# The q projection of two chunks as one Strassen pair, laid around an output projection

## The chip, the cores and the metric

The kernel runs on one core of a Trainium2 chip. A core has a matrix engine (TensorE, PE in the profile; PEld is its weight load), a vector engine (VectorE, DVE), a scalar engine (ScalarE, ACT), a general engine (GpSimd, POOL) and a sync engine (SyncE, SP) that issues most transfers. [...] The metric is the device time of one execution in microseconds, the median of three; lower is better.

## The reference

One transformer layer over 2,048 rows of 1,024 values: attention over a sliding, dilated window of 8 positions, then a gated feed-forward block. Both add to their input.

```python
def _A_ref(x, wqkv, wo):                      # S = 2048, D = 1024, 32 heads of 32
    qkv = (x @ wqkv) -> q, k, v per head
    idx = pos[:, None] - 2 * arange(8)        # the row itself and 7 earlier ones, two apart
    logits = einsum("bhsd,bhswd->bhsw", q, k[idx]) * 32 ** -0.5     # masked before row 0
    o = einsum("bhsw,bhswd->bhsd", softmax(logits), v[idx])
    return o @ wo

def _B_ref(x, w_gate, w_up, w_down):          # F = 3584
    return ((x @ w_gate) * (x @ w_up)) @ w_down

h  = x + _A_ref(layernorm(x), wqkv, wo)
h2 = h + _B_ref(layernorm(h), w_gate, w_up, w_down)
```

Inputs and output are bf16. What the change touches is the q third of `x @ wqkv`, for rows 1024 to 2047.

## The kernel before

The rows are cut into four chunks of 512 (`TC`). For each chunk the normalized rows lie transposed in `lnTs[c]` (128 x 8 x 512); wqkv is in six blocks of 512 columns: blocks 0 and 1 are q, 2 and 3 are k, 4 and 5 are v. One group is eight matmuls of 128x512, and each result is copied out by ScalarE and stored to memory, from where attention gathers it back with heads and positions over the partitions (qD, kD, vD).

```python
    def mm_group(ps, wt, j, rhs):
        for ko in range(KO):                                   # KO = 8
            nc.tensor.matmul(ps[:], lhsT=wt[:, ko, bass.ts(j, 128)], rhs=rhs[:, ko, :],
                             start=(ko == 0), stop=(ko == KO - 1))

    def qkv(c, blocks, last=False):
        for b in blocks:
            for j in range(4):
                ps = psum.tile([128, TC], F32, tag="mm", name=f"ps{c}_{b}_{j}")
                mm_group(ps, wts["qkv", b], j, lnTs[c])
                evac_qkv(c, b * 4 + j, ps)                     # ScalarE copy, store
                bg.step(GROUP_US)
            if last:
                retire()                                       # frees the weight buffer: the next weights load
```

The attention itself runs on VectorE, as a generator. A small planner, `bg`, puts pieces of it between the matmul groups while the program is written: each `yield` says what the piece is thought to cost, and `bg.step` hands out as much as a group of matmuls takes (`GROUP_US` is 1.73). So the order of the instructions on VectorE is fixed in the program; when they run depends on the chip.

```python
    def attention(c):
        while c and c - 1 not in over:
            yield "later", 1.0
        qD, kD = qkv_in["q", c], qkv_in["k", c]
        lg = att.tile([128, W, SUB], F32, tag="lg", name=f"lg{c}")
        for wp in range(W // 2):
            prod = att.tile([128, 2, DH, SUB], BF, tag="prod", name=f"prod{c}_{wp}")
            for j in range(2):
                o = HB - DIL * (2 * wp + j)
                nc.vector.tensor_tensor(prod[:, j], qD[:], kD[:, :, o:o + SUB], ALU.mult)
                yield 2.3
            # ... five folds of prod into the logits lg
        # ... softmax over lg; products with vD, summed into oD
        nc.gpsimd.dma_start(od[c].rearrange("c g d s -> (c g) d s"), oD[:])
        oT = att.tile([128, KO, 4, SUB], BF, tag="oT", name=f"oT{c}")
        for cp in range(4):
            nc.gpsimd.dma_start(oT[:, :, cp, :], od[c][cp].rearrange("(hg hl) d s -> (hl d) hg s", hl=4))
        oTs[c] = oT
        over.add(c)
        # ... loads for the next chunk
```

The output projection of chunk 0 multiplies oT by wo, adds the input rows and takes the second norm, on VectorE; chunk 1 does the same through `wo_norm`, which has the norm on ScalarE.

```python
    def wo_ln2(c, at={}):
        # ... norm(t): normalize(hs[t]) on VectorE, then a transposing DMA into lnT
        for t in range(4):
            for hf in range(2):
                ps = psum.tile([128, 512], F32, tag="mm", name=f"wo{c}_{hf}_{t}")
                # ... eight matmuls: oT by wo
                nc.vector.tensor_tensor(hs[t][:, bass.ts(hf, 512)], ps[:], hs[t][:, bass.ts(hf, 512)], ALU.add)
                if hf == 1:
                    stats(hs[t], mv4, t)                       # two bn_stats, one bn_aggr
                    rstd_of(mv4, rs4, t, t + 1)
                    bg.spend(1.5)
                elif t > 0:
                    norm(t - 1)
        # ...
```

The main line of this part, in order:

```python
    qkv(0, range(1, 4))                     # block 0 of chunk 0 was done at the start
    load_qk(0)
    bg.finish(rows2)
    for t in range(4):
        norm1[2].transpose(t)
    xtiles[3] = load_x(3, "x", nc.sync)
    pump(6)
    # ...
    start_attention(0)
    # ...
    qkv(1, range(4))
    qkv(0, range(4, 6))
    load_v(0)
    # ...
    qkv(1, range(4, 6))
    start_attention(1)
    pump(pair_at)
    qkv(2, range(6))
    start_attention(2)
    hss[0] = load_x(0, "h", nc.sync)
    qkv(3, range(4), last=True)
    bg.finish(atts[0])
    # ...
    nxt = wo_ln2(0)
    qkv(3, range(4, 6), last=True)
    start_attention(3)
    # ...
    hT0 = ffn1_first(nxt[0], {(4, 2): wo_1})                   # gate and up products; output projection 1 inside
```

The feed-forward part of chunks 2 and 3 already uses this scheme of seven products (`pair_block`), and so do the down products; they are not changed.

Of the kernel before, what the change touches and what calls it, by code (L numbers as in the profile page):

```python
# [18 lines left out]
D = 1024  # L19
# [59 lines left out]
def kernel(  # L79
# [46 lines left out]


# [72 lines left out]
    def load_x(c, what, eng):  # L200
        tiles = []
        for t in range(4):
            xt = hp.tile([128, D], BF, tag="h", name=f"{what}{c}_{t}")
            eng.dma_start(xt[:], x[bass.ds(c * TC + t * 128, 128), :])
            tiles.append(xt)
        return tiles
# [52 lines left out]
    class NormOnScalar(Norm1):  # L259
# [16 lines left out]
        def devs(self):  # L276
            nc.scalar.activation(self.nm, self.s, ACTF.Copy, scale=-1.0 / D)
            for t in range(4):
                nc.scalar.activation(self.junk[:], self.xs[t][:], ACTF.Square, bias=self.nm[:, t:t + 1],
                                     accum_out=self.ss[:, t:t + 1])  # L280
                yield "later", self.pace
            nc.scalar.activation(self.rs4[:], self.ss, ACTF.Ln, bias=eps[:], scale=1.0 / D)
# [17 lines left out]
        def rows(self):  # L300
            for t in range(4):
                self.row(t)
                self.transpose(t)
                yield "later", self.pace

# [33 lines left out]

    qkv_in = {}  # L340

    def evac_qkv(c, m, ps):
        sg = t1k.tile([128, HB + TC], BF, tag="t1k", name=f"sg{c}_{m}")
        nc.scalar.copy(sg[:, HB:HB + TC], ps[:])  # L344
# [5 lines left out]
        if m < 8:  # L350
            nc.sync.dma_start(qd[c][:, 4 * hg:4 * hg + 4, :, :].rearrange("c g d s -> (g d) c s"),
                              sg[:, HB:HB + TC].rearrange("p (c s) -> p c s", c=4))
# [81 lines left out]
    def qkv(c, blocks, last=False):  # L434
        for b in blocks:
            for j in range(4):
                ps = psum.tile([128, TC], F32, tag="mm", name=f"ps{c}_{b}_{j}")
                mm_group(ps, wts["qkv", b], j, lnTs[c])
# [9 lines left out]
    def load_qk(c):  # L448
        qD = att.tile([128, DH, SUB], BF, tag="qD", name=f"qD{c}")
        kD = att.tile([128, DH, SUB + HB], BF, tag="kD", name=f"kD{c}")  # L450
        nc.gpsimd.dma_start(qD[:], qd[c].rearrange("c g d s -> (c g) d s"))
# [98 lines left out]
    class Norm2(NormOnScalar):  # L550
# [11 lines left out]
        def finish(self):  # L562
            yield from self.devs()
# [5 lines left out]
    def wo_norm(c):  # L569
# [4 lines left out]
        for t in range(4):  # L574
            for hf in range(2):
# [6 lines left out]
                if hf == 0 and t > 0:  # L582
                    n.sum(t - 1)
                bg.step(GROUP_US)
        n.sum(3)
        retire(2)
        return n

    def wo_ln2(c, at={}):
        lnT = lnTp.tile([128, KO, TC], BF, tag="lnT", name=f"lnT2_{c}")  # L590
        hs = hss[c]
        mv4, rs4 = ln_tiles(f"2_{c}")

        def norm(t):
            ln = normalize(hs[t], mv4, rs4, t)
            nc.sync.dma_start_transpose(lnT[:, :, bass.ts(t, 128)], ln[:])

        for t in range(4):
            for hf in range(2):
                ps = psum.tile([128, 512], F32, tag="mm", name=f"wo{c}_{hf}_{t}")  # L600
                for kk in range(KO):
                    nc.tensor.matmul(ps[:], lhsT=oTs[c][:, kk, t, :], rhs=wts["wo", c, hf][:, kk, :],
                                     start=(kk == 0), stop=(kk == KO - 1))
                nc.vector.tensor_tensor(hs[t][:, bass.ts(hf, 512)], ps[:], hs[t][:, bass.ts(hf, 512)], ALU.add)
                if hf == 1:
                    stats(hs[t], mv4, t)
                    rstd_of(mv4, rs4, t, t + 1)
                    bg.spend(1.5)
                elif t > 0:
                    norm(t - 1)  # L610
                    bg.spend(0.55)
                bg.spend(0.7)
                if 2 * t + hf in at:
                    at[2 * t + hf]()
                bg.step(GROUP_US)
        norm(3)
        retire(2)
        for t in range(4):
            rows = hsd[c][:, t, :]
            nc.sync.dma_start(rows, hs[t][:, D - rows.shape[-1]:D])  # L620
        return lnT, hs

    ones = const.tile([128, 128], BF)
    nc.vector.memset(ones[:], 1.0)

    class Scale:
        def __init__(self, name, n):
            self.name, self.n = name, n  # L630
            self.l1 = const.tile([128, n], F32, name="l1" + name)
            self.rowb = const.tile([128, 1], BF, name="rowb" + name)

        def add(self, k, src, junk):
            nc.scalar.activation(junk, src, ACTF.Abs, accum_out=self.l1[:, k:k + 1])

        def rows(self):
            row = small.tile([128, 1], F32, tag="l1row", name="row" + self.name)
            nc.vector.tensor_reduce(row[:], self.l1[:], mybir.AxisListType.X, ALU.add)
            nc.vector.tensor_copy(self.rowb[:], row[:])  # L640

        def total(self, ps=None):
            n = TC if ps else 64
            ps = ps or psum.tile([128, TC], F32, tag="mm", name="l1ps" + self.name)
            nc.tensor.matmul(ps[:, 0:n], lhsT=ones[:], rhs=self.rowb[:].to_broadcast((128, n)), start=True, stop=True)
            tot = const.tile([128, 1], F32, name="tot" + self.name)
            nc.vector.tensor_copy(tot[:], ps[:, 0:1])
            eb = const.tile([128, 1], I32, name="eb" + self.name)
# [705 lines left out]
```

## Time and profile before

| | |
|---|---|
| time, median of 3 runs | 770.61 us (770.46 to 770.74) |
| span of the profiled execution | 768.7 us, 10,302 instructions |
| TensorE clock granted | 1.000 |
| TensorE busy | 762.8 us, 3,663 matmuls |
| VectorE busy | 606.0 us |
| ScalarE busy | 513.1 us |
| transfers | 144.85 MB, mean 188 GB/s |

The page of a profile lists the busy time of each engine, the chain of work that ended last (followed back from the last instruction, at each step to what released it), and groups of like instructions. In a group's line stand the source line, the engine, the operation, what is written and read, shapes and count, then busy time and mean duration of one, then the idle time before them and who ended it. A timeline row has the start, the duration, the engine and line, the operation, and in square brackets the idle time before it with what ended that. In the chain, pieces have a start, a length, an engine and a tile. In a list of waits, each line says who waited for whom: total, times, longest. A matmul's row shows 0.38 us because matmuls overlap; the distance between two of them is what counts.

### The profile page before, as it was taken

The numbers are of one execution on the slowest core, as the hardware profiler recorded it, in microseconds if no ns is written. First come the engines' busy times: TensorE is split into PE (matmuls) and PEld (weight loads), VectorE is DVE, ScalarE is ACT, GpSimd is POOL, SyncE is SP. The second block draws the span as 40 slices with busy tenths as digits, with TensorE's granted clock in tenths as the row PEclk, the third lists the DMA queues.
The fourth block names the chain that finished last, engine by engine and source line by source line (L and its number), as shares of the span: only waits on it lengthen the run. The fifth ranks groups of instructions, "written<-read, shape, count | busy, mean of one in ns | idle before, by whom it ended". The sixth has DMA issues, their size and how long they took to land.

```text
span 768.7 us, 10302 instructions
## 1 busy us (share of the span) xinstructions
PE 762.8 (99%) x3663; PEld 350.7 (46%) x3663; DVE 606.0 (79%) x718; ACT 513.1 (67%) x979; POOL 142.5 (19%) x152
## 2 busy tenths in 40 slices
PE   8999999999999999999999999999999999999998
PEld 5444444444444444444444444444444444444444
DVE  5639999999999999999998997975454444568863
ACT  4648966423687398778899986736777677788240
POOL 0000000200002000020000001018778677600000
PEclk9999999999999999999999999999999999999999
DMA  8999796999966699579559448674342423730001
GB/s 268 272 257 260 207 269 153 279 305 283 301 219 216 210 299 294 172 246 326 194 186 300 139 155 279 126 198 107 80 110 55 110 74 91 257 126 29 0 29 55
DMA packets 190915, 144.85 MB, mean 188 GB/s; under 512 B 81808, under 2 KB 181136, under 8 KB 188688
## 3 DMA queue, kind: packets, MB, share of 16 engines
q1 hardware_dynamic: 180416, 116.94, 54.2%
q0 software_dynamic: 3584, 22.02, 8.4%
q10 hardware_dynamic: 6864, 5.24, 2.5%
q8 instruction: 28, 0.46, 0.2%
q14 instruction: 23, 0.19, 0.1%
HBM read 110.10 MB, written 27.26 MB: 179 GB/s over the span
## 4 chain that ended last, share of the span: by engine, by line
PE 97%; DVE 2%; DMA 1%; issue 0%; ACTq 0%; DVEq 0%
PE ps L431 21%; PE dx L944 6%; PE pz L826 6%; PE pwu L431 6%; PE pu L431 6%; PE py L826 6%; PE pwg L431 6%; PE pg L431 6%; PE px L826 6%; PE wo L998 4%; PE pv L826 3%; PE ez L944 3%; PE ey L944 3%; PE ex L944 3%; PE dy L944 3%; PE wo L578 2%
## 5 line engine op out<-in xcount | busy, mean ns | idle before, releaser
L431 PE MATMUL ps<-lnT,w_qkv 128*128 128x512 bf16 x736 | 159.5, 379 | 0.0
L431 PEld LDWEIGHTS <-w_qkv 128*128 128x128 bf16 x736 | 71.9, 98 | 86.1 <-issue 0.2
L344 ACT CAST sg<-ps 128x512 bf16<-128x512 f32 x96 | 55.2, 586 | 46.9 <-PE ps L431 41.6
L477 DVE TENSOR_TENSOR prod<-qD,kD 128x4096 bf16<-128x4096 bf16 x32 | 72.2, 2284 | 12.8 <-DMA kD<-kd 12.8
L523 DVE TENSOR_TENSOR pv<-vD,at 128x4096 bf16<-128x4096 bf16 x32 | 72.4, 2285 | 0.2
L826 PEld LDWEIGHTS <-sw 128*128 128x128 f16 x448 | 43.8, 98 | 52.9 <-issue 0.2
L431 PEld LDWEIGHTS <-w_wu 128*128 128x128 bf16 x448 | 43.8, 98 | 52.9
L431 PEld LDWEIGHTS <-w_wg 128*128 128x128 bf16 x448 | 43.8, 98 | 52.9
L826 PE MATMUL px<-lnT,ws 128*128 128x512 bf16 x224 | 55.2, 379 | 0.0
L536 POOL DMA_DIRECT2D od<-oD x4 | 2.2, 544 | 275.6 <-DVE oD L534 275.6
L431 PE MATMUL pg<-lnT,w_wg 128*128 128x512 bf16 x224 | 52.9, 379 | 0.0
L431 PE MATMUL pu<-lnT,w_wu 128*128 128x512 bf16 x224 | 52.9, 379 | 0.0
L431 PE MATMUL pwu<-lnT,w_wu 128*128 128x512 bf16 x224 | 52.9, 379 | 0.0
L431 PE MATMUL pwg<-lnT,w_wg 128*128 128x512 bf16 x224 | 52.9, 379 | 0.0
L826 PEld LDWEIGHTS <-ws 128*128 128x128 f16 x336 | 32.9, 98 | 39.6
L807 POOL TENSOR_TENSOR sw<-ws 128x512 f16<-128x512 f16 x26 | 30.0, 1155 | 82.4 <-PE pv L826 49.1
L944 PEld LDWEIGHTS <-gs 128*128 128x128 f16 (+1 forms) x280 | 27.4, 98 | 33.0
L479 DVE TENSOR_TENSOR prod<-prod 128x4096 bf16<-128x4096 bf16 x16 | 36.6, 2288 | 0.4
L843 ACT COPY py<-px 128x512 f32<-128x512 f32 x28 | 16.0, 570 | 27.7 <-PE px L826 27.7
L808 POOL TENSOR_TENSOR sw<-sw,ws 128x512 f16<-128x512 f16 x26 | 30.0, 1154 | 2.0
L810 POOL TENSOR_TENSOR sw<-ws,sw 128x512 f16<-128x512 f16 x26 | 30.3, 1167 | 0.0
L809 POOL TENSOR_TENSOR sw<-ws 128x512 f16<-128x512 f16 x26 | 30.1, 1156 | 0.0
(334 smaller groups left out, 1472.9 us busy)
## 6 DMA issues: line engine op xcount, KB each, us to landing
w_wg<-in_B_w_gate_dram SPq DMA_DIRECT2D x14, 1024.0 KB, 6.9
w_wu<-in_B_w_up_dram SPq DMA_DIRECT2D x14, 1024.0 KB, 6.3
w_pair<-in_B_w_gate_dram SPq DMA_DIRECT2D x14, 512.0 KB, 4.0
w_pair<-in_B_w_up_dram SPq DMA_DIRECT2D x14, 512.0 KB, 5.3
w_wo<-in_A_wo_dram SPq DMA_DIRECT2D x6, 1024.0 KB, 7.6
w_qkv<-in_A_wqkv_dram SPq DMA_DIRECT2D x5, 1024.0 KB, 11.5
kd<-sg SPq DMA_DIRECT2D x32, 144.0 KB, 4.4
kD<-kd POOLq DMA_DIRECT2D x4, 1152.0 KB, 8.6
```

What stands on the lines that cost most here:

```text
L344: nc.scalar.copy(sg[:, HB:HB + TC], ps[:])
L431: nc.tensor.matmul(ps[:], lhsT=wt[:, ko, bass.ts(j, 128)], rhs=rhs[:, ko, :], start=(ko == 0), stop=(ko == KO - 1))
L477: nc.vector.tensor_tensor(prod[:, j], qD[:], kD[:, :, o:o + SUB], ALU.mult)
L479: nc.vector.tensor_tensor(prod[:, :, 0:16], prod[:, :, 0:16], prod[:, :, 16:32], ALU.add)
L523: nc.vector.tensor_tensor(pv[:, j], vD[:, :, o:o + SUB], at[:, w, None, :].to_broadcast((128, DH, SUB)), ALU.mult)
L807: eng.tensor_tensor(sw[:, i, 0], a21, a22, ALU.add)
L808: eng.tensor_tensor(sw[:, i, 1], sw[:, i, 0], a11, ALU.subtract)
L809: eng.tensor_tensor(sw[:, i, 2], a11, a21, ALU.subtract)
L810: eng.tensor_tensor(sw[:, i, 3], a12, sw[:, i, 1], ALU.subtract)
L826: nc.tensor.matmul(ps[:], lhsT=lhs[:, ko, :], rhs=rhs[:, ko, :], start=(fresh and ko == 0), stop=(ko == 3), skip_group_check=not fresh)
L944: nc.tensor.matmul(ps[:, bass.ds(lo, n)], lhsT=lhs[k][:, bass.ts(q, 128)], rhs=rhs[k][:, bass.ds(lo, n)], start=(fresh and k == 0), stop=( ...
L998: nc.tensor.matmul(ps[:], lhsT=oTs[c][:, kk, t, :], rhs=wts["wo", 2, hf][:, kk, :], start=(kk == 0), stop=(kk == KO - 1))
```

## The change

A product of two matrices, each cut into 2 x 2 blocks, needs eight block products; Strassen's scheme (here in Winograd's form) needs seven and some sums. The change computes the q projection of chunks 2 and 3 together in that way: the blocks of the weights are q columns m and 4 + m (blocks 0 and 1 of wqkv, `r`) by halves of the contraction (`kh`), and the blocks of the rows are chunks 2 and 3 by the same halves. Its aim is to save TensorE one eighth of these matmuls.

- The q weights are brought into f16 with a power-of-two scale (`Scale`, from a sum of absolute values over the weights), and sums of their blocks are made (`q_weight_sums`), all while chunk 0 and chunk 1 are projected. Chunk 1's q uses the scaled weights as well, so the order of chunk 1 becomes k, then q.
- Loads that stood beside the gather of attention 0's keys (transposes of chunk 2, rows of chunk 3, the v weights) are moved behind it: a tiny GpSimd copy makes the x load wait for kD, and qD waits for the transposes of chunk 1.
- Sums of the rows of chunks 2 and 3 (`q_row_sums`) are made on VectorE right behind attention 0; the last of them, T3, inside the pair, in a weight buffer (`room_q`).
- Half of the pair (m 0 and 1) is put in front of output projection 0, the other half behind it, with pieces of the last value block between its products.
- The norm after output projection 0 goes from VectorE to ScalarE (`wo_norm(0, devs=False)`; `wo_ln2` is removed).
- The total for another scale (`total_h1`) is taken two steps later in output projection 2.

```diff
+    def q_convert():
+        for r in range(2):
+            wt = wts["qkv", r]
+            nc.vector.tensor_scalar(f16(wt[:]), wt[:], scale_q.s, None, ALU.mult)
+        bg.spend(2.6)
+        bg.add(q_weight_sums(), bg.now)
+    def q_weight_sums():
+        for m in range(4):
 ... (a11, a12, a21, a22: the four f16 blocks of m; s1 to s4: rooms of 128x512)
+            nc.vector.tensor_tensor(s1, a21, a22, ALU.add)
+            nc.vector.tensor_tensor(s2, s1, a11, ALU.subtract)
+            nc.vector.tensor_tensor(s3, a11, a21, ALU.subtract)
+            nc.vector.tensor_tensor(s4, a12, s2, ALU.subtract)
+            yield 1.7
+    def q_row_sums():
+        while 0 not in over:
+            yield "later", 0.5
 ...
+        for k in range(4):
+            nc.vector.tensor_tensor(t1[k], b12[:, k, :], b11[:, k, :], ALU.subtract)
+            nc.vector.tensor_tensor(t2[k], b22[:, k, :], t1[k], ALU.subtract)
+            if k % 2:
+                yield 1.7
+        for k in range(4):
+            nc.vector.tensor_tensor(t4[k], b21[:, k, :], t2[k], ALU.subtract)
+        yield 1.7
+        def last_sum(room):
 ... (t3: a view of half of room)
+            nc.vector.tensor_tensor(t3, b22, b12, ALU.subtract)
+            bg.spend(1.3)
+    def q_product(ps, lhs, rhs, fresh):
+        for ko in range(4):
+            nc.tensor.matmul(ps[:], lhsT=lhs[:, ko, :], rhs=rhs[ko], start=(fresh and ko == 0), stop=(ko == 3),
+                             skip_group_check=not fresh)
+        bg.step(GROUP_US / 2)
+    def q_pair(m0, room, between=()):
 ... (out_scalar: ScalarE, scaled, and store; out_vector: VectorE, scaled plus p5, and store)
+        for i in two:
+            xb[i] = bank("x", i)
+            q_product(xb[i], a11[i], b11, True)
+            yb[i] = bank("y", i)
+            nc.scalar.copy(yb[i][:], xb[i][:])
+        for i in two:
+            v = bank("v", i)
+            q_product(v, sw[i][0], t1, True)
+            p5[i] = room[:, i, :]
+            nc.scalar.activation(p5[i], v[:], ACTF.Copy, scale=inv)
+        if m0 == 0:
+            qsum["t3"] = qsum["t3"](room)
+        t3 = qsum["t3"]
+        for i in two:
+            q_product(yb[i], sw[i][1], t2, False)
+            zb[i] = bank("z", i)
+            nc.scalar.copy(zb[i][:], yb[i][:])
+        for f in between[0:1]:
+            f()
+        for i in two:
+            q_product(xb[i], a12[i], b21, False)
+            out_scalar(2, m0 + i, xb[i])
+            q_product(zb[i], sw[i][2], t3, False)
+            ub[i] = bank("u", i)
+            nc.scalar.copy(ub[i][:], zb[i][:])
+            out_vector(3, 4 + m0 + i, zb[i], p5[i])
+        for f in between[1:2]:
+            f()
+        for i in two:
+            q_product(yb[i], sw[i][3], b22, False)
+            out_vector(3, m0 + i, yb[i], p5[i])
+            q_product(ub[i], a22[i], t4, False)
+            out_scalar(2, 4 + m0 + i, ub[i])
-    qkv(0, range(1, 4))
-    load_qk(0)
+    qkv(0, [1, 2], at={(1, 1): lambda: q_abs(0), (1, 2): lambda: q_abs(2), (1, 3): lambda: q_abs(1),
+                       (2, 0): lambda: q_abs(3), (2, 2): scale_q.rows})
+    qkv(0, [3], at={(3, 2): scale_q.total, (3, 3): q_convert})
+    load_qk(0, after=lnTs[1][:, 0, TC - 1:TC])
+    start_attention(0)
+    qkv(1, [2])
     bg.finish(rows2)
+    xtiles[3] = load_x(3, "x", nc.sync, after=qkv_in["k", 0][:, 0, 0:1])
+    pump(6)
+    state["live"] += 1
     for t in range(4):
         norm1[2].transpose(t)
 ...
-    qkv(1, range(4))
+    qkv(1, [3, 0, 1])
 ...
-    qkv(2, range(6))
+    qkv(2, range(2, 6))
+    rows_q = q_row_sums()
+    bg.add(rows_q, bg.now, first=True)
+    qkv(3, [2, 3], last=True)
+    hss[0] = load_x(0, "h", nc.sync)
+    state["live"] += 1
+    qkv(3, [4], last=True)
+    bg.finish(atts[0])
+    bg.finish(rows_q)
+    room_q = wpool.tile([128, 4, TC], F32, tag="w", name="room_q")
+    q_pair(0, room_q)
 ...
+    norm2 = [wo_norm(0, devs=False)]
+    norm2.append(norm2[0].finish(devs=False))
+    bg.add(norm2[1], bg.now, first=True)
+    qkv(3, [5], js=(0, 1))
+    q_pair(2, room_q, between=(lambda: qkv(3, [5], js=(2,)), lambda: qkv(3, [5], last=True, js=(3,))))
+    bg.finish(norm2[1])
```

`q_abs` sums absolute values of half a q block: halves 0 and 1 by a VectorE reduce (128x2048 to 128x1), 2 and 3 on ScalarE. Not shown: the bodies of `Scale` (moved, not changed), the loop parameters `at` and `js` of `qkv`, and the pace of `abs_down`, which goes from 4.9 to 3.9 groups.

## The prediction

> **What bounds the kernel now.** I read the page's share table first, then the chain of work that ended last, then that chain between 20 and 200 us, and last VectorE's timeline and waits around the first attention.
>
> ```profile
> PE 762.8 (99%) x3663; PEld 350.7 (46%) x3663; DVE 606.0 (79%) x718; ACT 513.1 (67%) x979; POOL 142.5 (19%) x152
> ...
> PE 97%; DVE 2%; DMA 1%; issue 0%; ACTq 0%; DVEq 0%
> ```
>
> ```profile
> 27.20 136.41 PE ps L431 x632
> 163.61 13.81 PE wo L602 x64
> 177.42 13.81 PE ps L431 x64
> 191.24 1.73 PE pg L431 x8
> ```
>
> TensorE holds 97% of the chain, and from 27.2 to 191.2 us (the stretch that the change rewrites) it never waits: 632 matmuls in 136.41 us are 0.2158 us each, and each 64 after them take 13.81 us, the same rate. So every matmul removed here is worth 0.2158 us, and every wait put in here costs its full length.
>
> VectorE is the second engine to watch, because attention lives on it:
>
> ```profile
> 39.02 0.55 DVE L192 TENSOR_SCALAR ln<-x,mv,rs 128x1024 bf16<-128x1024 bf16 x1 [1.64 <-ACT sg L347]
> 52.34 2.29 DVE L477 TENSOR_TENSOR prod<-qD,kD 128x4096 bf16<-128x4096 bf16 x1 [12.77 <-DMA kD<-kd]
> ```
>
> ```profile
> 134.26 2.29 DVE L534 TENSOR_TENSOR oD<-oD,pv 128x4096 bf16<-128x4096 bf16 x1
> 136.59 2.29 DVE L477 TENSOR_TENSOR prod<-qD,kD 128x4096 bf16<-128x4096 bf16 x1
> ```
>
> The reader is to see two things. VectorE is idle for 12.77 us before attention 0, until the gathered keys (kD) land. From 52.34 us on it runs attention 0 without a pause worth naming and ends it at 136.6: 84.25 us. Nothing on TensorE sets that end; the landing of kD does.
>
> ```profile
> 44.12 0.54 POOL L452 DMA_DIRECT2D kD<-kd  x1 [12.56 <-DMA kd<-sg]
> ```
>
> That load is issued at 44.12 us, when the last key block has been stored, and lands 8.2 us later.
>
> [...]
>
> **The change part by part.**
>
> Matmuls. The plain q projection of chunks 2 and 3 is 2 chunks x 8 blocks x 8 matmuls = 128. The pair computes four m, each in 7 products of 4 matmuls = 112. That is 16 fewer, 16 x 0.2158 = 3.45 us. The scale adds one 64-column matmul; a 128-column one takes 1.50 / 24 = 0.06 us in the chain. Net -3.39 us. All else on TensorE is the same work in another order, so without a new wait the answer would be 770.61 - 3.39 = 767.2.
>
> Preparation on VectorE, put into the idle stretch. [...] Behind the last norm come five tiny operations (about 0.8 us), two conversions of 128x4096 (1.28 us each by the row of the later gate/up conversion, 2.5 together) and 16 sums of 128x512. Independent ones follow each other at 4.78 / 14 = 0.34 us (row of 14 f16 sums at 441.58), one that reads the result just before it at about 0.45; four groups make 5.9. That is 9.2 us into a hole of 12.8. But the two ScalarE sums (1.9 us each by the row of the same operation on w_ring) push ScalarE's evacuations and norm factors about 2 us late, so the last norm ends at 40.0 rather than 39.5, and the weight sums at about 49.2.
>
> Start of attention 0. The last key block is stored about 1.7 us later than before, for the same ScalarE reason; its landing and kD's are quicker, because transposes, x and weight loads are now held behind kD. I take 1.2 us off the landing of that store and 2.2 off kD's 8.2, both guesses: 44.1 + 1.7 - 1.2 = 44.6 for the issue, and 6 us more, 50.6. So attention 0 starts at max(49.2, 50.6), say 50.3, some 2 us earlier than before, and ends at 50.3 + 84.25 = 134.5.
>
> The row sums. In the order of the built program VectorE does, behind attention 0: one product of attention 1 (2.24), the twelve 128x512 row sums of T1, T2, T4 (4.55), then a product (2.3), a fold (2.32), four smaller folds (1.26, 1.26, 0.72, 0.35), another product (2.24), and only then T3 (128x2048, 1.25). T1, T2 and T4 are there at 134.5 + 6.8 = 141.3. T3 is there 18.5 us behind attention 0, at 153.0.
>
> When TensorE wants them. Counting the matmuls in the new order from the same start, the first product of the pair begins at 143.0, the one with T1 at 144.7, the one with T2 at 146.4 and the one with T3 (the z product) at 149.0. T1, T2 and T4 are in time by 3 us. T3 is not: 153.0 - 149.0 = 4.0 us of wait. I lower it to 3.5, as VectorE's start could be up to a microsecond earlier.
>
> Output projection 0 comes at 155.2 instead of 163.6. Its oT follows the end of attention 0 by some 15 us (store 4.2, four gathers issued over 3.55, up to 7.5 to land), so 149.5: in time. Its own weights are loaded earlier too.
>
> Norm 2 of chunk 0 moves from VectorE (8 bn_stats at 0.65 and 4 norms at 0.5, about 7 us) to ScalarE. There, between 173 and 189 us, ScalarE has two sums over the last rows (2.6), four rows of 1.24 us, and the pair's copies and outputs of about 0.57 to 0.69 each. I follow them in order to a last row at about 188.5 and its transpose landed near 192; the gate products want it at 187.9 plus the 3.5 of above, 191.4. Expected loss 0.4 us, from nothing to 1.5.
>
> Attention 1 ends about 2 us later than before (row sums, T3 and the pair's outputs on VectorE, 4.6 + 1.3 + 8 x 0.70, less the 7 us that left, less the earlier start), near 239. Before, it ended at 237.4 and the first gather landed well before 253.4; now the first is due by about 251 and wanted at 250.0 + 3.5. Just in time.
>
> Sum: -3.39 + 3.5 + 0.4 = +0.5, or 771.1. I round to 771.0.
>
> **The rivals.** (1) No new wait: T3 comes in time, 767.2. For it: the order of the change is plainly laid out to keep kD's way free, and ScalarE's and VectorE's new work fits into measured holes. Against it: attention 0 would have to start at 46 us, while the weight sums alone keep VectorE until 49. (2) The wait is longer, or a second one joins it: kD lands no earlier than before (52.3), which makes the wait for T3 6 us, or the norm rows on ScalarE make the first gate product wait 1.5 to 2 us more. Then 772 to 774. For it: ScalarE is the only engine that gets both the norm and the pair's copies. Against it: a long wait for T3 gives slack to everything behind it. (3) The fifth weight block, now loaded behind kD, comes late for its matmuls at 67 us (issue near 54, 12.5 us to land as before). That would not add up: TensorE would only wait there instead of for T3, as VectorE goes on meanwhile.
>
> **Range and chances.** The end is set by T3, which is set by attention 0's start: 49.0 to 52.3 makes the wait 2.6 to 6 us, the time 769.8 to 773.2, and the norm rows add up to 1.5. I give rival 1 about 15%, and a wait of under 2 us another 15%. Predicted 771.0, 768.0 to 773.5. Two per cent are 15.4 us, more than four times what is removed, and no wait I see is near that: 0.98 within 2%.
>
> **What would show it.** The page should have 15 fewer matmuls (3,648). VectorE's timeline should show weight sums up to about 49, the first attention product at 50, its end near 134.5 and the 128x2048 subtraction ending near 153. TensorE's timeline should show one gap of 2 to 5 us ahead of a z product at 149, released by VectorE, and perhaps a small one at the first gate product, released by the transposing DMA. I am wrong if TensorE runs through 149 without a gap, if the first gap comes at the first gate product or at output projection 1, or if attention 0 starts before 48 or after 52.

## The result, and the profile after

| | before | after |
|---|---|---|
| time, median (four runs each) | 770.56 us (770.46 to 770.74) | 777.69 us (776.51 to 779.00) |
| ratio of the times | | 1.0093, 95% interval 1.0075 to 1.0110 |
| span of the profiled execution | 768.7 us | 775.9 us |
| first gate product starts | 191.07 us | 198.29 us |
| from there to the end | 577.6 us | 577.6 us |
| attention 1's output sent (od) | 237.41 us | 246.03 us |

The change saves its 16 matmuls and costs 7.1 us all the same, against the 0.5 us that the prediction added up. The last row but one places it: behind the first gate product the two executions are equally long, so everything happens before 198 us. The later total of the other scale, which the change also moves, therefore costs or brings nothing that can be seen.

The page of the changed kernel, busy time and the chain of work that ended last:

```profile
PE 759.5 (98%) x3592; PEld 349.8 (45%) x3648; DVE 622.1 (80%) x750; ACT 535.6 (69%) x1013; POOL 144.3 (19%) x154
...
PE 76%; DVE 3%; ACT 1%; issue 1%; DVEq 0%
```

The weight loads (PEld) count 3,648, the predicted number of matmuls (some matmul records are missing from this trace). VectorE has 16 us more to do than before, ScalarE 22 us. In the kernel before TensorE had 97% of the chain; now the chain passes through VectorE and ScalarE too. (The second line adds up to 81%, so part of the chain is not named there, and its 76 can't be set against the 97.) TensorE's list of waits says where (who waited for whom; total, times, longest, in us):

```profile
PE qz L945 <- DVE room_q L932: 6.9, 1, 6.9
...
PE ps L482 <- ACT halo L401: 0.8, 1, 0.8
PE qy L945 <- ACT qy L977: 0.5, 1, 0.5
...
PE ps L482 <- ACT room_q L982: 0.3, 1, 0.3
```

The first is the wait for T3 that the prediction had, at twice its size. VectorE's timeline of the changed kernel, the end of the weight sums, the start of attention 0, its last addition, and T3, followed by the row of GpSimd that asks for kD:

```profile
48.40 0.42 DVE L911 TENSOR_TENSOR qs<-w_qkv,qs 128x512 f16<-128x512 f16 x1
53.94 4.49 DVE L533 TENSOR_TENSOR prod<-qD,kD 128x4096 bf16<-128x4096 bf16 x2 [5.11 <-DMA kD<-kd]
...
135.80 2.29 DVE L590 TENSOR_TENSOR oD<-oD,pv 128x4096 bf16<-128x4096 bf16 x1
...
155.51 1.22 DVE L932 TENSOR_TENSOR room_q<-lnT 128x2048 f16<-128x2048 bf16 x1
```

```profile
46.77 0.54 POOL L508 DMA_DIRECT2D kD<-kd  x1 [9.13 <-DMA kd<-sg]
```

The weight sums end at 48.8 as predicted, and then VectorE stands idle for 5.1 us: kD is asked for at 46.8 and lands at 53.9. Attention 0 takes 84.2 us from there, and T3 ends 18.6 us behind it, both as predicted, so T3 is out at 156.7 and not at 153.0. The chain between T3 and the gate product (start, length, who, how many):

```profile
155.60 1.14 DVE room_q L932
156.79 1.89 PE qz L945 x4
158.68 1.47 PE qx L945 x4
160.15 0.86 PE qz L945 x4
...
198.46 1.73 PE pg L482 x8
```

Four matmuls take 0.86 us; the first four behind the wait take 1.89, the next four 1.47. That is 1.6 us more, and the table of stretches of the same kernel shows why (stretch, its length, TensorE's busy time and matmuls, granted clock, share of the DMA engines, GB/s):

```profile
150.00:152.00 2.00, 0.00 (x0) 1.00 1.20 330
152.00:154.00 2.00, 0.00 (x0) 0.74 1.08 241
154.00:156.00 2.00, 0.00 (x0) 0.50 1.13 272
156.00:158.00 2.00, 1.21 (x3) 0.50 1.04 348
158.00:160.00 2.00, 2.00 (x7) 0.55 0.99 357
160.00:162.00 2.00, 2.00 (x11) 1.00 1.13 346
```

TensorE goes idle at 149.9, its granted clock falls from 1.00 to 0.50 at about 153, and it comes back some 3 us after work has started again: 3.1 us from the start of the wait to the half clock, and 3.0 us back.

The account of the span then reads: 3.4 us saved; 6.9 for T3; 1.6 for the clock; 0.8 at 111 us, where TensorE waits for ScalarE to copy a result out of one of the kernel's eight accumulator tiles (`psum`), as ScalarE stood still for 6.55 us up to 110; 1.2 between 178 and 190, where ScalarE is behind. That is +7.1, and the spans differ by 7.2.

### The profile page after: what moved, and what is told of

It is laid out like the page before. It is cut to its first block, busy times and chain, and to the rows that moved or that the text cites. A ratio compares the mean times of both kernels' runs of the same rounds, so it can differ in the third digit from the quotient of the medians.

```text
span 775.9 us, 10279 instructions
## 1 busy us (share of the span) xinstructions
PE 759.5 (98%) x3592; PEld 349.8 (45%) x3648; DVE 622.1 (80%) x750; ACT 535.6 (69%) x1013; POOL 144.3 (19%) x154
## 4 chain that ended last, share of the span: by engine, by line
PE 76%; DVE 3%; ACT 1%; issue 1%; DVEq 0%
PE dx L1088 6%; PE pz L830 6%; PE pwu L482 6%; PE pu L482 6%; PE py L830 6%; PE pg L482 6%; PE pwg L482 6%; PE px L830 6%; PE wo L647 4%; PE wo L1142 4%; PE pv L830 3%; PE ez L1088 3%; PE ey L1088 3%; PE ex L1088 3%; PE dy L1088 3%; PE ev L1088 2%
## 5 line engine op out<-in xcount | busy, mean ns | idle before, releaser
L482 PE MATMUL ps<-lnT,w_qkv 128*128 128x512 bf16 x595 | 131.7, 379 | 1.8 <-ACT halo L401 0.8
L482 PEld LDWEIGHTS <-w_qkv 128*128 128x128 bf16 (+1 forms) x608 | 59.3, 98 | 72.4 <-issue 1.7
L396 ACT CAST sg<-ps 128x512 bf16<-128x512 f32 x72 | 41.7, 587 | 19.0 <-PE ps L482 9.3
L830 PE MATMUL px<-lnT,ws 128*128 128x512 bf16 x212 | 53.1, 379 | 0.6
L482 PE MATMUL pwg<-lnT,w_wg 128*128 128x512 bf16 x219 | 52.3, 379 | 0.2
L811 POOL TENSOR_TENSOR sw<-ws 128x512 f16<-128x512 f16 x26 | 29.9, 1152 | 86.3 <-PE pv L830 52.7
```

The source lines that it names most:

```text
L830: nc.tensor.matmul(ps[:], lhsT=lhs[:, ko, :], rhs=rhs[:, ko, :], start=(fresh and ko == 0), stop=(ko == 3), skip_group_check=not fresh)
```

## The experiments

Each is the changed kernel with one edit, timed beside the kernel before. This table has what the discussion below rests on: the four TensorE waits (at the z product, which is for T3 except for the 0.3 us of e14 to e17; at the qy product of the second half, for ScalarE; at the first gate product, for a transposed row; at output projection 1, for attention 1's output), and when attention 0 starts, the first gate product starts and attention 1's output is sent. Times are medians, the rest is from the profiled executions.

| run | time (us) | ratio to before, 95% | z | qy | gate | proj. 1 | att. 0 | gate at | output 1 |
|---|---|---|---|---|---|---|---|---|---|
| before | 770.56 | | | | | | 52.3 | 191.1 | 237.4 |
| after | 777.69 | 1.0075 to 1.0110 | 6.9 | 0.5 | 0 | 0 | 53.9 | 198.3 | 246.0 |
| e1 | 775.93 | 1.0050 to 1.0102 | 0 | 2.3 | 4.5 | 0 | 54.1 | 198.1 | 247.3 |
| e2 | 775.70 | 1.0046 to 1.0079 | 0.5 | 0.5 | 0 | 0 | 54.0 | 196.9 | 244.7 |
| e3 | 779.88 | 1.0102 to 1.0132 | 6.4 | 0.5 | 0 | 0 | 56.0 | 201.2 | 249.0 |
| e4 | 775.06 | 1.0042 to 1.0075 | 4.9 | 0.5 | 0 | 0 | 51.0 | 195.4 | 243.1 |
| e5 | 774.48 | 1.0030 to 1.0060 | 0 | 1.9 | 3.6 | 0 | 51.9 | 193.2 | 241.1 |
| e6 | 792.98 | 1.0272 to 1.0308 | 6.5 | 0 | 0 | 6.1 | 52.0 | 196.3 | 253.0 |
| e7 | 790.09 | 1.0231 to 1.0262 | 0 | 1.1 | 0 | 8.7 | 52.7 | 189.1 | 248.1 |
| e8 | 773.89 | 1.0026 to 1.0055 | 0 | 0.8 | 3.6 | 0 | 51.7 | 193.0 | 241.1 |
| e9 | 774.18 | 1.0037 to 1.0062 | 0 | 2.1 | 3.6 | 0 | 53.5 | 194.9 | 243.0 |
| e10 | 776.89 | 1.0071 to 1.0102 | 6.9 | 0.5 | 0 | 0 | 52.1 | 198.0 | 245.7 |
| e11 | 774.58 | 1.0039 to 1.0064 | 0 | 0.7 | 3.6 | 0 | 51.6 | 192.8 | 242.0 |
| e12 | 782.14 | 1.0131 to 1.0177 | 0 | 2.1 | 0 | 4.4 | 52.3 | 191.4 | 245.4 |
| e13 | 777.27 | 1.0065 to 1.0099 | 0 | 1.7 | 2.3 | 3.3 | 53.7 | 193.6 | 247.5 |
| e14 | 781.83 | 1.0125 to 1.0176 | 0.3 | 2.5 | 0 | 5.6 | 51.7 | 192.5 | 247.0 |
| e15 | 781.06 | 1.0124 to 1.0154 | 0.3 | 0.5 | 0 | 5.5 | 51.6 | 189.7 | 244.9 |
| e16 | 781.43 | 1.0113 to 1.0149 | 0.3 | 0.5 | 0 | 5.5 | 54.8 | 190.9 | 246.0 |
| e17 | 781.09 | 1.0120 to 1.0152 | 0.3 | 0.5 | 0 | 5.5 | 51.4 | 189.8 | 244.9 |
| e18 | 772.27 | 1.0013 to 1.0026 | 0 | 2.7 | 0 | 0 | 52.1 | 192.3 | 232.6 |

### Is it T3, the clock, or kD? (e1 to e4)

e1 moves T3 to its place right behind T1 and T2, in other memory:

```diff
+        t3at = f16(att.tile([128, W, SUB], BF, tag="at", name="t3at")[:].rearrange("p w s -> p (w s)"))
+        t3 = [t3at[:, bass.ts(k, TC)] for k in range(2)]
+        t3 += [t1k.tile([128, TC], F16, tag="t1k", name=f"qt3_{k}")[:] for k in range(2)]
+        for k in range(4):
+            nc.vector.tensor_tensor(t3[k], b22[:, k, :], b12[:, k, :], ALU.subtract)
 ... (last_sum and its call inside the pair are taken out)
```

> T3 (b22 - b12, the operand of the z product) is computed right behind T1 and T2 in other memory, ahead of attention 1's pieces on VectorE, nothing left out. Theory (the z product waits for T3, and the clock drops because of that wait): T3 is out near 145.5, well before TensorE wants it at 149.9; the wait of 6.9 us and the slow qz and qx products (1.6 us) both go, 769.2 us (768.2 to 770.5). Rival A (most of the loss lies elsewhere, in ScalarE's norm and the loads, and the wait only moves to a later product): 773 to 777 us, with a new TensorE wait of some us after 150. Rival B (the wait goes, the slow clock stays): 770.8 us.

775.93 us: the wait for T3 is gone and almost nothing is won. Rival A held: 2.3 us now stand at the qy product, 4.5 at the first gate product, and that product starts at 198.1 as in the changed kernel. Part of it is my edit: ScalarE sat idle 8.8 us until 163 for a staging tile (a `t1k` buffer), and e1 uses two of these for T3. e5 mends that.

e2 puts 30 matmuls that nobody reads into the wait:

```diff
+            if m0 == 0 and i == 0:
+                fill = bank("f", 0)
+                for _ in range(30):
+                    nc.tensor.matmul(fill[:], lhsT=a11[0][:, 0, :], rhs=b11[0], start=True, stop=True)
             q_product(zb[i], sw[i][2], t3, False)
```

> The changed kernel with 30 matmuls of 128x512 (0.2158 us each, 6.5 us) whose product nobody reads, put just ahead of the z product, where TensorE otherwise stands idle for 6.9 us. Theory (the qz and qx products behind the wait are slow because an idle TensorE is granted a lower clock): those groups come back to 0.86 us, 776.1 us (775.5 to 776.8) though 30 matmuls more are computed. Rival (they are slow because of what they read, or because of the instruction queue): 777.7 us or more, groups still 1.5 to 1.9 us.

775.70 us, and the two stretches that stood at half clock, from the same table for e2:

```profile
156.00:158.00 2.00, 1.45 (x8) 1.00 1.02 358
158.00:160.00 2.00, 2.00 (x11) 1.00 1.00 343
```

30 matmuls more make the kernel 2.0 us faster by the medians (the ranges of the two overlap by 0.6 us), and the granted clock is 1.00 where it was 0.50 and 0.55: the slow products were the clock, and the clock was the wait. The gate product starts 1.35 us earlier than in the changed kernel.

e3 takes away what holds q's load back, `load_qk(0)` in place of `load_qk(0, after=...)`; this was my explanation of kD's late landing.

> The changed kernel with the load of q of chunk 0 not held back until chunk 1's transposes are in; all else equal. Theory (kD lands at 53.9 instead of 50.6 because the 1 MB of q moves at the same time as the stores of k): q moves near 31 to 37, kD lands at 50.5 to 51.5, attention 0 and T3 are 2.5 to 3.4 us earlier, the wait at 149.9 shrinks to 3.5 to 4.4 us, 774.5 us (773.8 to 775.3). Rival (kD is late because ScalarE evicts k late): kD lands after 53, 777 to 778 us.

779.88 us: the theory fell, and in the other direction. Attention 0 starts at 56.0, later than in any other run. TensorE's list of waits for e3:

```profile
PE qz L945 <- DVE room_q L932: 6.4, 1, 6.4
PE ps L482 <- ACT halo L401: 1.9, 1, 1.9
PE ps L482 <- DMA lnT<-ln: 1.3, 1, 1.3
```

The third line is new. With q's load let loose, chunk 1's transposes come late, TensorE waits for them, and the stores of k follow TensorE. The gate protects kD's way; it doesn't block it.

e4 leaves two of the four sums of absolute values out of the scale, those on ScalarE:

```diff
-    scale_q = Scale("q", 4)
+    scale_q = Scale("q", 2)
-    qkv(0, [1, 2], at={(1, 1): lambda: q_abs(0), (1, 2): lambda: q_abs(2), (1, 3): lambda: q_abs(1),
-                       (2, 0): lambda: q_abs(3), (2, 2): scale_q.rows})
+    qkv(0, [1, 2], at={(1, 1): lambda: q_abs(0), (1, 3): lambda: q_abs(1),
+                       (2, 2): scale_q.rows})
```

> The changed kernel with the scale taken from two half blocks alone: ScalarE's two sums of absolute values (2.1 us each) are left out of the computation. Theory (these sums push ScalarE's evictions of k, and so the stores and kD, by about 2 us): kD lands at 51.5 to 52.3, 775.7 us (775.0 to 776.5). Rival (kD is set by the q load[...]): kD within 0.5 us of 53.9, 777.2 to 778 us.

775.06 us. GpSimd's row for e4:

```profile
44.46 0.54 POOL L508 DMA_DIRECT2D kD<-kd  x1 [8.64 <-DMA kd<-sg]
```

kD is asked for at 44.5 in place of 46.8, and attention 0 starts at 51.0: here kD comes nearly as the prediction wanted it. So ScalarE's two sums make kD late, as e4's theory had it. By how much, one trace can't tell. Thirteen profiled executions (after and twelve of the runs) have the same instructions up to here, and attention 0 starts anywhere from 51.7 to 54.8 in them; in the four whose four sums are all on VectorE (e8, e11, e15, e17) it starts at 51.4 to 51.7. So the sums cost kD anything from next to nothing to some 3 us; why equal programs differ by that much is not shown. And where it starts at 53.5 or later, the wait at 111 us is 0.65 to 2.1 us; where it starts before 52.7, it is 0.4 or nothing. The change makes the x load wait for kD, so the transposes of chunk 3 do, and ScalarE, which has a weight load (w_ring) to issue there, waits for these (it stands idle for 6.55 us up to 110 in the changed kernel). The change moves these weight loads as well (the pace of `abs_down`); no run takes the two apart. But even with kD at 51.0 T3 comes 4.9 us late, and the kernel is 4.4 us slower than the one before.

### Is it ScalarE's norm? (e5 to e8)

e5 is e1 with T3 in the `at` buffer and in one norm row's buffer, so that no staging tile is taken:

```diff
+        for h, (pool, tag) in enumerate(((att, "at"), (lnp, "ln"))):
+            t = f16(pool.tile([128, D], BF, tag=tag, name=f"t3_{h}")[:]).rearrange("p (k s) -> p k s", k=2)
+            nc.vector.tensor_tensor(t, b22[:, bass.ts(h, 2), :], b12[:, bass.ts(h, 2), :], ALU.subtract)
 ... (t3 is filled from these; last_sum and its call inside the pair are taken out)
```

> T3 right behind T1 and T2 as in e1_t3_early, but kept in the attention weights' buffer and one norm row's buffer, so that ten staging tiles are left for evictions as in the changed kernel (e1 took two of them). Theory now: e1's 8.8 us of ScalarE idling at 163 (a staging tile held by a store of v) was made by my own use of two staging tiles; without it ScalarE's norm runs from about 161 to 186, its last transposed row is in near 191.5, the first gate product waits 0 to 2 us, and the rest of the gain stays: 771 us (770 to 772.5). Rival (the stores of v back up in any case, and ScalarE's chain of norm and evictions sets the gate product whatever T3 does): gate product not before 196, 774 to 777 us.

774.48 us: by the time the rival's, but the gate product starts at 193.2, earlier than it said. The wait of 6.9 us is gone, and 5.5 us of waits stand elsewhere. TensorE's waits for e5, then ScalarE's timeline where the norm begins:

```profile
PE pg L482 <- DMA lnT<-ln: 3.6, 1, 3.6
PE qy L945 <- ACT qy L977: 1.9, 1, 1.9
```

```profile
157.98 0.69 ACT L961 ACTIVATE sg<-qu,ibq 128x512 bf16<-128x512 f32 x1 [4.26 <-DMA vd<-sg]
163.08 1.06 ACT L279 ACTIVATE njunk<-h 128x1024 bf16<-128x1024 bf16 x1 [4.41 <-DVE h L649]
```

ScalarE idles 4.3 us for a staging tile that a store of v still holds, and then 4.4 us for VectorE's additions of output projection 0. The norm begins at 163.1 although TensorE began that projection at 154.6. And behind the 3.6 us at the gate the clock drops again, to a granted 0.50 from 193 to 195: eight matmuls take 3.37 us in place of 1.89.

e6 puts the norm back on VectorE as in the kernel before (T3 late), e7 does it on top of e5:

```diff
-    norm2 = [wo_norm(0, devs=False)]
-    norm2.append(norm2[0].finish(devs=False))
-    bg.add(norm2[1], bg.now, first=True)
+    lnT2_0 = wo_ln2(0)[0]
```

> The changed kernel with the norm behind output projection 0 on VectorE as in the kernel before; T3 stays late. Theory: wait of 6.9 us and slow clock stay, ScalarE's 1.2 us of waits between 178 and 190 go, 776.5 us (775.8 to 777.2). Rival (VectorE, full of attention 1, is late with the norm): a wait for a transposed row at the first gate product, 778 us or more.

> e5 and e6 together. Theory (T3's place, the clock dip and ScalarE's norm are all of the loss but the 0.8 us at 111): 768.7 us (767.7 to 770), no TensorE wait over 0.6 us between 145 and 200. Rival 1 (another engine sets this stretch, the wait comes back elsewhere): 771 us or more. Rival 2 (VectorE's norm makes attention 1 late for output projection 1 near 255): a new wait there of 1 us or more.

792.98 and 790.09 us, the slowest of all. Both theories fell. e6's rival had the time right and the place wrong: no wait at the gate product, but 6.1 us at output projection 1. e7's second rival held: its gate product starts at 189.1, 2.0 us before that of the kernel before, so TensorE has more than half of the promised 3.4 us up to there. Then it waits 8.7 us at output projection 1 for attention 1's output, which leaves at 248.1, and from there to the end it takes 12 us longer than the runs that don't wait there: 2.7 for slower products behind that wait (63 on record in 16.71 us, where 64 take 13.98), 1.9 for VectorE's sums at 475, and 5.0 at output projection 3 for attention 3's output. The rest, some 2 us, I put down to slower products behind the last; that is an estimate. So what VectorE lost before 248 it hadn't made up by 478, when that output leaves (458.6 in the kernel before). In this order VectorE cannot carry the norm beside the new sums. Moving it to ScalarE was no side effect of the change but what makes it possible.

e8 has all four sums of absolute values on VectorE (`if k < 4` in `q_abs`) on top of e5:

> e5 with all four sums of absolute values on VectorE (2.25 us each) and none on ScalarE. Theory: kD lands near 51 as in e4, weight sums end near 51 to 52.5, attention 0 starts 1.5 to 2.5 us earlier than in e5, and the 0.8 us at 111 goes: e5 less 0.5 to 1.2 us. Rival (VectorE's later sums push the norm rows of chunk 1 or 2, and TensorE waits for a transposed row between 35 and 75): e5 plus 1 us or more.

773.89 us, e5 less 0.6 by the medians, and the ranges overlap. kD comes at 51.7, no earlier than the 51.9 of e5's own profile, which has no wait at 111 either; what changes is the qy product, which waits 0.8 for 1.9. TensorE waits 0.6 us for the later total, and the gate's 3.6 stays.

### Is it the staging tiles, or VectorE's order? (e9 to e17)

e9 stages the eight q blocks of the first half in attention 0's output buffer, so that no store of v can hold them up; e10 does that alone; e11 is e9 with e8's sums:

```diff
+        rows = att.tile([128, 8, TC], BF, tag="oD", name="q_rows") if m0 == 0 else None
+        slots = iter(range(8))
         def stage(c, m):
+            if rows is not None:
+                return rows[:, next(slots), :]
 ... (the copies out and their stores take these rows)
```

> e5 with the eight evicted q blocks of the first Strassen pair staged in attention 0's output buffer (free once its store has landed) in place of the staging tiles shared with v, whose stores are held up in SyncE's queue from 143 to 154. Theory (what is left of e5's loss is one chain: stores of v hold staging tiles, so evictions on ScalarE and VectorE wait to 158, so ScalarE's norm begins at 163 and not near 159, so the qy product waits 1.9 us and the first gate product 3.6 us and runs 1.5 us slow after it): norm begins near 159, both waits go or fall below 0.6 us each, 768 us (767 to 769.5), below the kernel before. Rival (ScalarE has too much to do between 159 and 187 whatever its start): the norm begins earlier, but gate product still waits 2 us or more, 771 to 774 us.

> The changed kernel with that staging alone, T3 late as it was. Theory: T3's wait of 6.9 us gives the stores of v the time they need, so the staging is worth nothing by itself: 777.5 us (776.5 to 778.3), T3's wait 6 to 7 us. Rival (the staging tiles are the real trouble, T3 second): 775.5 us or less.

> e9 with all four sums of absolute values on VectorE as in e8. Theory: ScalarE's sums cost only what kD's landing costs, and that is off the path once T3 is early; e9 less 0 to 0.8 us. Rival: the later total makes TensorE wait 0.6 us as in e8 and gains nothing: e9 plus 0 to 0.6 us.

774.18, 776.89 and 774.58 us. e10 did as expected, and e11 is level with e9, as its rival said. e10 also shows that attention 0's start alone doesn't set the wait for T3. It starts 1.8 us earlier than in the changed kernel, and the wait is as long, from 148.7 to 155.6:

```profile
155.61 1.89 PE L949 MATMUL qz<-room_q,qs 128*128 128x512 f16 x4 [6.87 <-DVE room_q L936]
```

TensorE, which has no wait at 111 here, comes 1.2 us earlier as well, and VectorE loses 0.6 of the 1.8 inside attention 0. e9's theory fell: the stall at 158 is gone and the norm begins no earlier. ScalarE's timeline for e9:

```profile
164.84 1.06 ACT L279 ACTIVATE njunk<-h 128x1024 bf16<-128x1024 bf16 x1 [7.82 <-DVE h L653]
```

All the idling is now "<-DVE h": VectorE adds output projection 0 at 163.5, because some 10 us of attention 1's pieces stand ahead of it in VectorE's order. It is the same thing that makes T3 late: from 145 on VectorE's order is about 7 us behind TensorE's. So e12 changes one number, by which attention 1 is held back behind T4:

```diff
             nc.vector.tensor_tensor(t4[k], b21[:, k, :], t2[k], ALU.subtract)
-        yield 1.7
+        yield 8
```

e13 and e14 do it on top of e5 (6 and 8), e15 is e14 with e8's sums, e16 is e14 with e9's staging, e17 has all three.

> The changed kernel with one number changed: behind the last row sum (T4), attention 1's pieces are held back by 8 us of VectorE's time in place of 1.7 us. T3 then stands behind one piece of 2.3 us and not behind seven of 10.2 us, q's combinations and the additions of output projection 0 stand nearer to their products. Theory (VectorE's order is 7 us behind TensorE's, which makes T3 and the norm late alike): T3 ends near 148.6 to 149, no wait of over 0.6 us at 149.9, norm begins before 161, gate product waits 0 to 1 us: 768.5 us (767.2 to 770.2), below or level with the kernel before. Rival (ScalarE's norm is too long in itself): T3's wait goes but a gate wait of 2 us or more with slow clock stays, 773 to 775 us. Rival 2 (attention 1 ends later and output projection 1 waits for it): a new wait near 255, 771 to 775 us.

> e5 with attention 1 held back by 6 us in place of 1.7 us behind T4. Theory: h's first addition near 161, norm starts near 161.5, gate wait 0 to 1.5 us, 769.5 us (768 to 771). Rivals as for e12_hold8.

> e5 with attention 1 held back by 8 us behind T4. Theory: as e12_hold8 with T3 out of VectorE's queue by 145.4: 768.3 us (767.2 to 769.8), within 0.6 us of e12_hold8. Rival (T3's own place still matters): e12 at least 1.5 us slower than this.

> e14_t3_early_hold8 with all four sums of absolute values on VectorE. Theory (kD's landing no longer sets anything on the path, but a late landing can cost the 0.8 us at 111): within 0.7 us of e14, on either side. Rival (attention 1 is now on the path at output projection 1, so each us of attention 0's start counts): 1 us or more below e14.

> e14_t3_early_hold8 with the first pair's q blocks staged in attention 0's output buffer as in e9. Theory: VectorE's idling of 4.6 us near 155 to 159 goes, attention 1's output leaves near 241 to 242.5 in place of 247, output projection 1 waits 0 to 1 us, the qy wait falls below 1 us: 769.5 us (768 to 772). Rival (VectorE has too much work between 140 and 246 even without a stall): attention 1's output not before 244, a wait of 2.5 us or more at output projection 1, 775 us or more.

> e16 with all four sums of absolute values on VectorE. Theory: ScalarE's waits at the qy product of the second pair go (0.5 us in e15 against 2.5 us in e14), attention 0 starts within 0.5 us of e16's: e16 less 0 to 2 us. Rival: no difference of more than 0.5 us.

782.14, 777.27, 781.83, 781.06, 781.43 and 781.09 us. Half of the theory held: in e12 one number takes T3's wait away, the norm begins at 161.3, and no gate wait is left; in e15 and e17 the gate product starts at 189.7 and 189.8, 1.3 us before the kernel before. But e12 is 4.4 us slower than the changed kernel, and of the six only e13, which holds back least, is level with it. That is e12's second rival. e14 is level with e12, so T3's own place no longer matters there, and with e15, e16 and e17 within 1 us of e14 neither the sums nor the staging tiles do. TensorE's wait list and GpSimd's timeline for e17:

```profile
PE wo L651 <- DMA oT<-od: 5.5, 1, 5.5
```

```profile
244.88 0.54 POOL L596 DMA_DIRECT2D od<-oD  x1 [42.55 <-DVE oD L594]
```

Attention 1's output leaves at 244.9, and output projection 1 can start 12.7 us behind it (store, gathers, landing), at 257.6; TensorE wanted it at 252.1. From output projection 1 to the end e17 then takes 521.3 us, against 515.4 in the runs that don't wait there: 1.4 for its slow first products (64 in 15.42 us for 13.98), a wait of 1.9 us for VectorE at 471, and 1.7 for slow products behind that (45 in 11.81 us; e12 has them in 10.12). The last 0.9 stays open. Not every wait is followed by slow products: the 64 matmuls of output projection 1 take 13.98 us in the kernel before; these are they in e12 (granted clock 0.50 to 0.51 from 257 to 263) and in e13.

```profile
258.13 16.36 PE L647 MATMUL wo<-w_wo,oT 128*128 128x512 bf16 x64 [4.40 <-DMA oT<-od]
```

```profile
260.90 13.99 PE L647 MATMUL wo<-w_wo,oT 128*128 128x512 bf16 x64 [3.28 <-DMA oT<-od]
```

e16 and e17 show that the stalls behind staging tiles aren't it: they are gone, and the output leaves at 246.0 and 244.9 (e16's rival). What is left is how much VectorE has to do.

### Take the work itself away (e18)

e18 leaves the sums T1 to T4 out of the computation; the products read chunk blocks in their place, and every matmul stays. The twelve staging tiles of the sums come free too.

```diff
-        t1, t2, t4 = ...                              # and the loops that compute them, and T3
-        qsum["b"] = (cells(b11), cells(b21), t1, t2, t4, cells(b22))
+        qsum["t3"] = cells(b12)
+        qsum["b"] = (cells(b11), cells(b21), cells(b12), cells(b22), cells(b21), cells(b22))
```

> The changed kernel with the row sums T1 to T4 left out of the computation: the Strassen products read b12, b22, b12 and b21 in their place, every matmul and every other operation stays (the 12 staging tiles of the sums are free as well). VectorE has 6.2 us less to do and TensorE nothing to wait for. Theory (the sums' 6 us of VectorE, in a stretch where VectorE has no slack, are what the change cannot pay): no wait for a sum, additions of output projection 0 in step with its products, norm begins near 159 to 161, attention 1's output leaves near 239 to 241 as TensorE needs it, 768 us (767 to 769.5), below the kernel before by 1 to 3.5 us. Rival (ScalarE's norm and the evictions are too much in any case): a gate wait of 2 us or more with slow clock, 771 to 774 us.

772.27 us, 5.4 us below the changed kernel and still 1.7 above the kernel before by the medians (ratio 1.0019, interval 1.0013 to 1.0026). By the time this is the rival's, but its wait for the gate product isn't there. GpSimd's timeline and TensorE's waits for e18:

```profile
232.64 0.54 POOL L592 DMA_DIRECT2D od<-oD  x1 [27.91 <-DVE oD L590]
```

```profile
PE qy L928 <- ACT qy L960: 2.7, 1, 2.7
```

Without the sums attention 1's output leaves 13.4 us earlier than in the changed kernel and 4.8 us earlier than in the kernel before: VectorE has slack again. (The twelve free staging tiles are a second difference of this run. e9 and e10, which eased the staging alone, gained 0.3 and 0.8 us, so I put the 5.4 down to VectorE's work; no run separates the two.) But the norm still begins at 163.2, since the planner filled the room with attention 1's pieces, and the qy product of the second half waits 2.7 us for ScalarE; the slow products behind it cost some 1.7 us more (granted clock 0.50 from 180 to 182). That eats the saving of 3.4. Whether e18 with attention held back would fall below the kernel before wasn't tried; nor was doing the row sums on GpSimd.

## Why the prediction was wrong

It said 771.0 (768.0 to 773.5) and the time is 777.7: the change costs 7.1 us where its sum had 0.5. Of the 6.6 between them 3.4 are at T3 (6.9 of wait for 3.5), 1.6 the clock behind that wait, 0.8 the wait at 111, and 0.8 ScalarE's norm (1.2 for 0.4). As a size, the start of attention 0 failed; as a mechanism, "The end is set by T3". By its own steps:

- **Matmuls, -3.39.** Right: 15 fewer weight loads.
- **Preparation on VectorE.** Right: the weight sums end at 48.8 for 49.2. The two reduces take 2.23 and 2.28 us.
- **Start of attention 0.** Here it failed: "I take 1.2 us off the landing of that store and 2.2 off kD's 8.2, both guesses: 44.1 + 1.7 - 1.2 = 44.6 for the issue, and 6 us more, 50.6." Measured are 46.8 and 7.2, so 53.9, past its own sign of being wrong (a start after 52). The working was also 0.3 loose: of 49.2 and 50.6 the larger counts, not 50.3. Of the two sums on ScalarE I had put their 1.7 us in and then taken most of it out again for loads held back. The runs show no such bonus at the issue: with the two sums left out (e4) it comes at 44.5, where the kernel before has 44.1. The landing did get quicker, by 1.0 and not by 2.2; that the loads held back are the reason was my estimate. At T3 this one term is 3.6 us: attention 0 ended at 138.1 and not at 134.5. Rival 2 had kD no earlier than 52.3 and a wait of 6 us; its 772 to 774 lacked the clock and the 0.8 at 111.
- **The row sums and when TensorE wants them.** Right in kind: T1, T2 and T4 in time, T3 18.6 us behind attention 0 for 18.5. TensorE wants it at 149.9 for 149.0; the 0.8 us at 111 that delays it is in no step of mine. It comes and goes with kD (e4 and the thirteen starts above), and so an earlier kD shortens the wait less than the prediction's sum says (e10).
- **A wait costs its length.** This is the second thing the sum lacked: 6.9 us of wait cost 8.5, because the clock drops to 0.50 (e2 keeps it at 1.00).
- **Norm 2 on ScalarE, 0.4.** Measured 1.2, and at the qy product and a v block, not at the gate. Against rival 2 it said that "a long wait for T3 gives slack to everything behind it", and e5 bears that out: with T3 in time, qy and gate wait 5.5 us together.
- **Attention 1 "near 239", projection 1 "just in time".** It left at 246.0; projection 1 didn't wait only because TensorE was 7 us late itself.
- **"The end is set by T3."** This was the error of thought, where the others are of size. T3's wait was the visible part of a shortage on VectorE. Take it away and the time falls by 3.2 us and not by 8.5 (e5); put VectorE's order right and TensorE waits for attention 1 (e12 to e17). From the end of attention 0 to attention 1's output VectorE needed 100.8 us in the kernel before (136.6 to 237.4), 104.9 in e5, 96.4 in e18 (of the 8.5 between these two, 6.4 is busy time). The row sums (6.0 us with T3) and eight outputs of 0.74 us outweigh the norm that left (8.2 us). In e17 output projection 1 starts 12.7 us behind that output (11.8 to 13.4 in the eight executions that waited there); by that the kernel before had 3.1 us to spare, and a TensorE 3.4 us faster wants it 3.4 us earlier. So, an estimate from these numbers and not shown by a run: 3.7 us more on VectorE and 3.4 less on TensorE are 7.1 against 3.1, a wait of 4.0 where 3.4 are saved. Even a perfect order with these sums on VectorE would end up about where the kernel before is.

None of the versions tried beats the kernel before; the nearest that computes everything is e8 (ratio 1.004, interval 1.0026 to 1.0055).

## What to carry to other kernels

Before matmuls are traded for sums, ask of the engine that gets the sums how much it has to spare up to its own next deadline, not only at the place where the sums stand; here VectorE was 97% busy from 54 to 237 us before the change, and what was put on it came out as a wait at whichever consumer was next. A wait that is removed tells by what it leaves behind: look at the next two consumers before counting it as won. And price a long TensorE wait above its length: the seventeen waits of 3.6 to 8.7 us at the z product, the gate and output projection 1 cost 1.4 to 2.7 us on top, in slower products behind them; the granted clock there is 0.50 in the changed kernel, e5 and e12.

## What the runs showed of the hardware

- Slow products also come after shorter waits, and not each time. Waits of 2.05 us (e12), 2.49 (e14) and 2.65 (e18) at the qy product and of 2.28 at the gate (e13) cost 1.7 to 1.8 us on top (the granted clock is 0.50 from 179 to 181 in e12 and from 180 to 182 in e18); 2.26 us (e1) and 2.07 us (e9) at the qy product cost at most 0.2, at a granted 1.00, and 3.28 us at output projection 1 in e13 cost nothing (its line is above). What decides between the two is not shown.
- A GpSimd copy of one column took 2.34 us at 53.93, where the same form took 0.19 us at 36.15. At 53.94 VectorE began a product of 2.29 us. The two durations are close; whether one held up the other is not shown. In the change this copy stands ahead of the x load, which is issued at 56.30, 2.4 us behind kD.
- Four stores of v, 144 KB each, took SyncE 10.95 us to issue from 142.86 on in e5 (the shortest such issue takes 0.36), with rows of h and a weight block in the same queue ahead of them. ScalarE's wait for a staging tile there ended with one of them (157.98, above).
